# Products of q and the state in four quarters of the TensorE array, with the outputs of a chunk in two PSUM banks

## The chip, the cores and the metric

The kernel runs on one core of a Trainium2 chip. The metric is the device time of one execution in microseconds (us). In the rows below the engines are PE (TensorE matmuls), PEld (TensorE weight loads), DVE (VectorE), ACT (ScalarE), POOL (GpSimd) and SP (SyncE, which issues most DMAs). Each engine works through its own instructions in order; semaphores make one wait for another.

## The reference, cut to what matters

Three stages follow each other. Only the first is touched by the change.

```python
# 1. recurrent attention: B=4 batches, H=8 heads, S=768 steps, D=48
for t in range(S):
    state = alpha[t][:, None] * state + outer(k[t], v[t])   # D x D for each batch and head
    y[t] = q[t] @ state
x = y.transpose(0, 2, 1, 3).reshape(3072, 384)
# 2. x @ w_in (384 x 2048), a leaky rectifier, @ w_out
# 3. ((x @ w1) * (x @ w2)) @ w3 @ w_out2
```

## The kernel before

**Chunks.** The 768 steps of a batch are cut into 6 chunks of 128, so there are 24 chunks, numbered 0 to 23. Inside a chunk the recurrence becomes matrix products. With q and k scaled by the running products of alpha (`prep`), the kernel forms for each head the 128 x 128 scores (`scores`), masks them on DVE (`sc`), and then has y = v x scores + state x q (`yout`), and the update of the state, k transposed x v (`state`). The 8 heads lie as 4 pairs `p` of two heads `hh`: head 2p in partitions 0 to 63, head 2p + 1 in 64 to 127, 48 of each 64 in use. These products are plain float32, and each one shows in the trace as two MATMUL and two LDWEIGHTS instructions, so that a group of 8 products is a row with x16.

**The four groups of products of a chunk n**, in the order in which `chunk` writes them: `state` (tile `Up`, 8 products of 64 columns, contraction over 128 partitions, outputs of the two heads of a pair in the two halves of the partitions), `yout` (tile `yp`: 8 products of v and `sc`, 128 columns, same shape; then 8 products of the state `sst` and `qt`, contraction over the 64 partitions of a head, output in the same 64 partitions, which are a quarter of the array on its diagonal; these are left out in the first chunk of a batch, n = 0, 6, 12, 18), and `scores` of chunk n + 1 (tile `scp`, contraction over 48 partitions, 128 x 128 outputs, one PSUM bank for each `hh`). The last chunk of a batch (n = 5, 11, 17, 23) has no `state`. The transposes of k (`kT`, tile `kTp`) are a unit of their own.

**PSUM banks.** Of the 8 banks two hold `h` of stage 2, and two rings of three are for the rest. While stage 2 accumulates tile T (512 tokens, 4 chunks) in one ring, the attention of tile T + 1 uses the other, whose banks `bank` gives out in turn. Before, a chunk takes five: `Up` one, `yp` one, `scp` two, `kTp` one. A bank is free again when its reader is done: `Up` is read by DVE (`tmp`, or `sst` in the first chunk of a batch), `yp` by ACT (the copy to `yT`), `scp` by DVE (`sc`), `kTp` by ACT (the copy to `kT`). At the end of a tile ACT copies the three accumulators out (`x1e`).

**Order.** Stage 2 runs in steps of 9 matmuls of `G1` (tile `h`) and 9 of `G2` (tile `acc`). After each `G1`, ACT makes `u` from `h`, DVE makes `g`, ACT makes `gs` from `g`, DVE the second half of `gs`. `attend` spreads the units of attention between the steps. Among ACT's other work are `top` (the upper halves of the weights of a later stage, which waits for a DMA into `raw`), and `r` twice (logarithm and exponential of `prep`, of which the first waits for DVE's scan of `al`). A scheduler sets the order of PE, ACT and DVE; `tight` keeps the products of a chunk in the order written, except that the first after `untie` is free to move. Tile 0 (chunks 0 to 3) is done ahead of stage 2; chunks 4 to 7 run beside stage 2 of tile 0, up to about 98 us, and chunks 8 to 23 beside the tiles after it, up to about 432 us. Stage 3 fills the rest and has no attention in it.

**Output.** ACT copies `yp` into `yT`, DMAs place its rows in the layout of x (`place`), and the host orders the rows of w_in to fit.

Of the kernel before, what the change touches and what calls it, by code (L numbers as in the profile page):

```python
# [24 lines left out]
CH = 128  # L25
NC_B = S // CH
NSTEP = B * NC_B
NP = H // 2
# [35 lines left out]
def fused_kernel(ctx, tc, qk, al, vv, wf, ws, m_alpha, ident, maskn, out):  # L64
# [6 lines left out]
    def copy(out, in_):  # L71
        act.activation(out=out, in_=in_, func=AF.Copy)  # L72
# [172 lines left out]
    def ends(n):  # L245
        return n % NC_B == NC_B - 1
# [28 lines left out]
    pairs = [(p, hh, slice(64 * hh, 64 * hh + DP)) for p in range(NP) for hh in range(2)]  # L275

    def state(n, w):
        if ends(n):
            return
        t, v, end = st.pop(("kT", n)), st["v", n], st.pop(("pend", n))  # L280
        ps = bank([128, NP, DP], "Up", w)
        for p, hh, r in pairs:
            mm(ps[r, p], t[:, p, r], v[:, 2 * p + hh], start=True, stop=True)
        new = sst[(n + 1) % 2]
        pend = end.to_broadcast([128, NP, DP])
        if n % NC_B == 0:
            dve.scalar_tensor_tensor(out=new, in0=ps, scalar=-1.0, in1=pend, op0=ALU.mult, op1=ALU.mult)
        else:
            tmp = ap2.tile([128, NP, DP], F32, tag="tmp", name="tmp", bufs=1)
            dve.tensor_tensor(out=tmp, in0=sst[n % 2], in1=ps, op=ALU.subtract)  # L290
            dve.tensor_tensor(out=new, in0=tmp, in1=pend, op=ALU.mult)

    def yout(n, w):
        qt, v = st.pop(("qt", n)), st.pop(("v", n))
        sc = [st.pop(("sc", n, hh)) for hh in range(2)]
        alone = n % NC_B == 0
        ps = bank([128, NP, CH], "yp", w)
        for p, hh, r in pairs:
            mm(ps[r, p], v[:, 2 * p + hh], sc[hh][:, p], start=p == 0, stop=alone and p == NP - 1,
                      skip_group_check=True)  # L300
        if not alone:
            for p, hh, r in pairs:
                mm(ps[r, p], sst[n % 2][r, p], qt[r, p], start=False, stop=p == NP - 1, skip_group_check=True)
        T, c = divmod(n, SPT)
        if c % 2 == 0:
            st["yT"] = ap2.tile([128, NP, 2, CH], F32, tag="yT", name="yT", bufs=1)
        y = st["yT"]
        copy(y[:, :, c % 2], ps)
        if c == 0:
            new_x(T)  # L310
        if c % 2 == 0:
            return
        x = f32(xt[T][:, 1, :, (c - 1) * CH:(c + 1) * CH])
        y = y.rearrange("p a c t -> p a (c t)")

        def place():
            q = (sp, act) if n == SPT - 1 else (sp, sp)
            for hh in range(2):
                q[hh].dma_start(out=x[hh * D:(hh + 1) * D], in_=y[64 * hh:64 * hh + D, :KD])
            for i, (k, to, hh, e, n_) in enumerate(PIECES):  # L320
                q[i % 2].dma_start(out=x[to:to + n_, k], in_=y[64 * hh + e:64 * hh + e + n_, KD])

        later(1, place)
# [10 lines left out]

    def chunk(n, w, more=True):
        untie()
        state(n, w)
        yout(n, w)
        if more:
            scores(n + 1, w)  # L340
        load_v(n + 3)
# [282 lines left out]
    with tc.If(bad > 0):  # L624
        with tc.tile_pool(name="fa", bufs=1) as fa:
# [5 lines left out]
            with tc.For_i(0, B, 1) as b:  # L631
                dve.memset(S_, 0.0)
                with tc.For_i(0, NC_B, 1) as c:
# [7 lines left out]
                    for g in range(CH // TG):  # L641
# [21 lines left out]
                            pe.matmul(yp, blk, z.rearrange("p a e -> p (a e)"), start=True, stop=True)  # L663
                            copy(yt[:, i].rearrange("p a e -> p (a e)"), yp)
                        dst = y_d[one][:, :, g * TG:(g + 1) * TG]
                        whole = [(k, hh * D, hh, 0, D, k) for k in range(KD) for hh in range(2)]
                        for k, to, hh, e, n_, a in whole + [piece + (KD,) for piece in PIECES]:
                            sp.dma_start(out=dst[:, :, :, k, to:to + n_].rearrange("b c t e -> (b c) t e"),
                                         in_=yt[hh:hh + 1, :, a, e:e + n_])

        with tc.tile_pool(name="fb", bufs=1) as fb:
            wi = fb.tile([128, NF, KD, 128], F32, name="wi")
# [95 lines left out]
```

## Time and profile before

| | us |
|---|---|
| three runs | 861.25, 860.70, 860.72 |
| median | 860.72 |
| the profiled execution | 860.4 |
| its span (first to last instruction) | 858.5 |
| PE busy in the span | 832.5 |
| DVE busy | 459.3 |
| ACT busy | 352.6 |

The profiled execution lies 0.3 us under the median, and 1.9 us of it lie around the span. The page has the busy time of each engine and the chain of work that ended last. Timelines give the instructions in order of time, merged into rows where equal ones follow each other; the time in brackets is how long the engine stood idle ahead of a row, and what released it.

### The profile page before, as it was taken

The page shows a single profiled execution, that of the slowest core. Times are in us where ns is not written, and L with a number is a line of the kernel's source. Part 1 is how long each engine was busy: PE and PEld are TensorE (multiplying, and loading weights), DVE is VectorE, ACT ScalarE, POOL GpSimd, SP SyncE. Part 2 cuts the span into 40 slices and gives each one's busy share as a digit, 9 for nine tenths or more (in the row PEclk, how much of TensorE's full clock was granted, in tenths as well). Part 3 has the DMA queues.
Part 4 walks back from the last instruction along what each step waited for, and adds up shares of the span by engine and source line. Part 5 has one row for each costly group of instructions (what it writes and reads, how often), then busy time and mean ns, then how long its engine had stood idle before and what let it go on. Part 6 is the DMA issues. An engine that isn't in the chain of part 4 may idle for free.

```text
span 858.5 us, 11862 instructions
## 1 busy us (share of the span) xinstructions
PE 832.5 (97%) x4754; PEld 685.2 (80%) x4758; DVE 459.3 (53%) x643; ACT 352.6 (41%) x538; POOL 11.9 (1%) x53
## 2 busy tenths in 40 slices
PE   7698999999999999999999999999999999999996
PEld 4477788888888888888888889988888888888884
DVE  7889974675576577656434734551433435322221
ACT  4456765444454545454335634421313232222221
POOL 1100000000000000000000000000000000000000
PEclk9989999999999999999999999999999999999998
DMA  8665662421573476436002405430312104010101
GB/s 311 186 227 203 210 214 79 139 80 54 213 245 107 147 251 228 158 102 213 13 19 92 141 0 192 143 108 1 106 41 74 74 14 134 1 37 0 37 1 41
DMA packets 48623, 99.55 MB, mean 116 GB/s; under 512 B 4784, under 2 KB 25008, under 8 KB 48560
## 3 DMA queue, kind: packets, MB, share of 16 engines
q1 hardware_dynamic: 48320, 98.52, 34.1%
q8 instruction: 39, 0.64, 0.3%
q10 hardware_dynamic: 240, 0.20, 0.1%
q14 instruction: 24, 0.20, 0.1%
HBM read 75.63 MB, written 18.35 MB: 109 GB/s over the span
## 4 chain that ended last, share of the span: by engine, by line
PE 89%; DVE 5%; DMA 3%; ACT 1%; issue 1%; SPq 1%; DVEq 0%; ACTq 0%
PE ab L361 23%; PE h L361 21%; PE acc L361 11%; PE acc L386 8%; PE acc L387 7%; PE acc L389 7%; PE w L361 4%; PE yp L237 3%; PE scp L237 2%; PE Up L237 1%; DMA raw<-in_ws_dram 1%; DMA raw<-in_wf_dram 1%; PE kTp L256 1%; DVE y L146 1%; DVE al L214 1%
## 5 line engine op out<-in xcount | busy, mean ns | idle before, releaser
L361 PE MATMUL h<-x,w 128*128 128x512 f32 x864 | 215.3, 393 | 5.5 <-ACT x L72 5.5
L361 PE MATMUL ab<-x,w 128*128 128x512 f32 x864 | 203.7, 389 | 0.0
L361 PEld LDWEIGHTS h<-x,w 128*128 128x128 f32 x864 | 162.5, 189 | 39.9 <-ACT x L72 6.0
L361 PEld LDWEIGHTS ab<-x,w 128*128 128x128 f32 x864 | 162.1, 188 | 33.6
L386 PE MATMUL acc<-gs,w 128*128 128x512 f32 x288 | 114.6, 398 | 0.0
L564 DVE TENSOR_TENSOR c<-ab,a 128x512 f32<-128x512 f32 x48 | 33.1, 691 | 149.0 <-PE ab L361 149.0
L387 PE MATMUL acc<-gs,w 128*128 128x512 f32 x288 | 112.4, 390 | 0.0
L375 DVE SCALAR_TENSOR_TENSOR g<-h,salpha,u 128x512 f32<-128x512 f32 x96 | 71.8, 748 | 71.0 <-ACT u L373 70.5
L373 ACT ACTIVATE u<-h,sgn 128x512 f32<-128x512 f32 x96 | 65.5, 682 | 103.4 <-PE h L361 103.3
L361 PE MATMUL acc<-cs,w 128*128 128x512 f32 x432 | 105.8, 389 | 0.0
L378 DVE SCALAR_TENSOR_TENSOR gs<-g,sgn,gs 128x512 fp32r<-128x512 f32 x96 | 72.0, 750 | 50.3 <-ACT gs L377 49.5
L361 PEld LDWEIGHTS acc<-cs,w 128*128 128x128 f32 x432 | 81.0, 188 | 17.2 <-DVE cs L567 0.4
L377 ACT ACTIVATE gs<-g,sgn 128x512 fp32r<-128x512 f32 x96 | 69.0, 719 | 52.9 <-DVE g L375 52.9
L389 PE MATMUL acc<-gs,w 128*128 128x512 f32 x288 | 81.0, 389 | 0.0
L72 ACT ACTIVATE a<-ab 128x512 f32<-128x512 f32 x48 | 28.8, 599 | 113.7 <-PE ab L361 113.7
L72 ACT ACTIVATE cs<-c 128x512 fp32r<-128x512 f32 x48 | 30.2, 630 | 89.7 <-DVE c L564 89.7
L386 PEld LDWEIGHTS acc<-gs,w 128*128 128x128 f32 x288 | 54.0, 188 | 12.3 <-issue 0.2
L389 PEld LDWEIGHTS acc<-gs,w 128*128 128x128 f32 x288 | 54.1, 188 | 11.4
L387 PEld LDWEIGHTS acc<-gs,w 128*128 128x128 f32 x288 | 54.1, 188 | 10.6
L72 ACT ACTIVATE top<-raw 128x768 f16<-128x768 bf16 (+1 forms) x39 | 41.8, 1072 | 42.2 <-DMA raw<-in_ws_dram 25.6
L567 DVE TENSOR_TENSOR cs<-c,cs 128x512 fp32r<-128x512 f32 x48 | 33.2, 692 | 30.8 <-ACT cs L72 30.8
L146 DVE SCALAR_TENSOR_TENSOR y<-raw,top 128x768 int32<-128x768 int32 (+1 forms) x39 | 36.9, 947 | 8.9 <-ACT top L72 6.0
(64 smaller groups left out, 654.7 us busy)
## 6 DMA issues: line engine op xcount, KB each, us to landing
raw<-in_ws_dram SPq DMA_DIRECT2D x22, 767.8 KB, 5.7
qk<-in_qk_dram SPq DMA_DIRECT2D x24, 512.0 KB, 5.9
raw<-in_wf_dram SPq DMA_DIRECT2D x16, 767.8 KB, 5.8
ws_d<-y SPq DMA_DIRECT2D x22, 384.0 KB, 2.8
al<-in_al_dram SPq DMA_DIRECT2D x24, 256.0 KB, 5.0
v<-in_vv_dram SPq DMA_DIRECT2D x24, 256.0 KB, 3.0
alx<-in_al_dram SPq DMA_DIRECT2D x8, 768.0 KB, 4.6
x_d<-x1e SPq DMA_DIRECT2D x18, 256.0 KB, 5.0
```

The costliest lines, as they stand in the source:

```text
L72: act.activation(out=out, in_=in_, func=AF.Copy)
L146: return dve.scalar_tensor_tensor(out=y, in0=t[:, :, 0], scalar=13, in1=z[:, :n], op0=ALU.logical_shift_right, op1=ALU.bitwise_or)
L237: ins = pe.matmul(*a, **k)
L361: pe.matmul(ps, w, x, start=first and i == 0, stop=last and i == n - 1)
L373: act.activation(out=u, in_=ps, func=AF.Identity, scale=sg)
L375: dve.scalar_tensor_tensor(out=gt, in0=ps, scalar=sa, in1=u, op0=ALU.mult, op1=ALU.max)
L377: act.activation(out=s[:, 0], in_=gt, func=AF.Identity, scale=sg)
L378: dve.scalar_tensor_tensor(out=s[:, 1], in0=gt, scalar=sg, in1=f32(s[:, 0]), op0=ALU.mult, op1=ALU.subtract)
L386: pe.matmul(acc[T][m], r_out[f][:, 0, c], s[:, 0], start=f == 0, stop=False)
L387: pe.matmul(acc[T][m], r_out[f][:, 1, c], s[:, 0], start=False, stop=False)
L389: pe.matmul(acc[T][m], r_out[f][:, 0, c], s[:, 1], start=False, stop=f == NF - 1)
L567: dve.tensor_tensor(out=s[:, 1], in0=c, in1=f32(s[:, 0]), op=ALU.subtract)
```

## The change

`yout` now comes ahead of `state` in a chunk. Its outputs take two banks of the ring instead of one: bank `hh` holds the outputs of the heads `hh` of all four pairs, pairs 0 and 2 in the lower half of the partitions, 1 and 3 in the upper (`a` is the half). The products of the state and q come first; each contracts over the 64 partitions of its head and writes to the half `a`, and the four of two pairs are one in each quarter of the array. The products of v and the scores follow, first all of bank 0, then all of bank 1. ACT's one copy of `yp` (512 columns) becomes two of 256 columns. A chunk thus takes six banks of the ring of three instead of five: `yp` two, `Up` one, `scp` two, `kTp` one, so that within a chunk `scp` follows `yp` in the same two banks, and `kTp` follows `Up`. The DMAs of `place` are as many as before; which head stands in which row of x, and the host's order of w_in, change with it.

```diff
     def state(n, w):
+        v, end = st.pop(("v", n)), st.pop(("pend", n))
         if ends(n):
             return
-        t, v, end = st.pop(("kT", n)), st["v", n], st.pop(("pend", n))
+        t = st.pop(("kT", n))
...
     def yout(n, w):
-        qt, v = st.pop(("qt", n)), st.pop(("v", n))
+        qt, v = st.pop(("qt", n)), st["v", n]
...
-        ps = bank([128, NP, CH], "yp", w)
-        for p, hh, r in pairs:
-            mm(ps[r, p], v[:, 2 * p + hh], sc[hh][:, p], start=p == 0, stop=alone and p == NP - 1,
-                      skip_group_check=True)
+        ps = [bank([128, NP // 2, CH], "yp", w) for _ in range(2)]
+        half = [slice(64 * a, 64 * a + DP) for a in range(2)]
         if not alone:
-            for p, hh, r in pairs:
-                mm(ps[r, p], sst[n % 2][r, p], qt[r, p], start=False, stop=p == NP - 1, skip_group_check=True)
+            for i in range(NP // 2):
+                for hh, a in ((0, 0), (1, 1), (0, 1), (1, 0)):
+                    mm(ps[hh][half[a], i], sst[n % 2][half[hh], 2 * i + a], qt[half[hh], 2 * i + a], start=i == 0, stop=False,
+                       skip_group_check=True)
+        for hh in range(2):
+            for i in range(NP // 2):
+                for a in range(2):
+                    pr = 2 * i + a
+                    mm(ps[hh][half[a], i], v[:, 2 * pr + hh], sc[hh][:, pr], start=alone and i == 0, stop=i == NP // 2 - 1,
+                       skip_group_check=True)
...
-        copy(y[:, :, c % 2], ps)
+        for hh in range(2):
+            copy(y[:, 2 * hh:2 * hh + 2, c % 2], ps[hh])
...
     def chunk(n, w, more=True):
         untie()
+        yout(n, w)
         state(n, w)
-        yout(n, w)
         if more:
             scores(n + 1, w)
```

The order that the scheduler gives moves with it. On PE, chunk 13 (the second of tile 3), before:

```order
L361 MATMUL h<-x,w_84 128x512 x9
L237 MATMUL Up<-v,kT 64x64 [waits DVE_49,Activation_49]
L237 MATMUL Up<-v,kT 64x64 x7
L237 MATMUL yp<-sc,v 64x128 [waits DVE_49]
L237 MATMUL yp<-sc,v 64x128 x7
L237 MATMUL yp<-qt,sst_113 64x128 x8
L237 MATMUL scp<-qt,kn 128x128 [waits PE_49]
L237 MATMUL scp<-qt,kn 128x128 [waits DVE_49]
L237 MATMUL scp<-qt,kn 128x128 x6
L386 MATMUL acc_2193<-gs,w_82 128x512
```

and with the change, at the same place:

```order
L369 MATMUL h<-x,w_84 128x512 x9
L237 MATMUL yp<-qt,sst_113 64x128 [waits DVE_49] x2
L237 MATMUL yp<-qt,sst_113 64x128 x6
L237 MATMUL yp<-sc,v 64x128 x8
L237 MATMUL Up<-v,kT 64x64 [waits Activation_49]
L237 MATMUL Up<-v,kT 64x64 x7
L237 MATMUL scp<-qt,kn 128x128 [waits Activation_49]
L394 MATMUL acc_2219<-gs,w_82 128x512
L237 MATMUL scp<-qt,kn 128x128 [waits Activation_49]
L237 MATMUL scp<-qt,kn 128x128 x6
```

The products of q and the state moved to the front, the second product of `scp` waits for ACT and no longer for DVE, and one matmul of `acc` stands between the first and the second of `scp`. This form, one of `scp`, one of `acc`, seven of `scp`, stands in chunks 9, 10, 13, 15, 19, 21 and 22 of 8 to 23; in chunk 14 two, and in chunk 18 one, of `acc` stand ahead of all 8 of `scp`.

On ACT, in chunk 13, before and then with the change:

```order
L72 ACTIVATE top<-raw 128x768 [waits DMAHW1_49,DVE_49]
L373 ACTIVATE u<-h,sgn 128x512 [waits PE_49,Activation_49]
L377 ACTIVATE gs<-g,sgn 128x512 [waits DVE_49]
L72 ACTIVATE yT<-yp 128x4x128 [waits PE_49]
L72 ACTIVATE top<-raw 128x768 [waits DMAHW6_49,DVE_49,Activation_49]
```

```order
L72 ACTIVATE top<-raw 128x768 [waits DMAHW1_49,DVE_49]
L381 ACTIVATE u<-h,sgn 128x512 [waits PE_49,Activation_49]
L72 ACTIVATE yT<-yp 128x2x128 [waits PE_49]
L385 ACTIVATE gs<-g,sgn 128x512 [waits DVE_49]
L72 ACTIVATE yT<-yp 128x2x128 [waits PE_49]
L72 ACTIVATE top<-raw 128x768 [waits DMAHW6_49,DVE_49,Activation_49]
```

The one copy became two, with `gs` between them; `top` and `u` stand ahead of both as they stood ahead of the one. In chunks 15, 19 and 22 it is `u`, copy, `gs`, copy, without a `top` right ahead; in 9 and 10 `r` twice stands ahead of `u`; in 14 it is `top`, `u`, `r`, `r`, `gs` and then both copies; in 21 `gs`, `top`, `u`, copy, `gs`, copy.

On PE, chunk 16 (the first of tile 4), before and then with the change:

```order
L361 MATMUL h<-x,w_83 128x512 x3
L237 MATMUL Up<-v,kT 64x64 [waits Activation_49]
L237 MATMUL Up<-v,kT 64x64 x7
L237 MATMUL yp<-sc,v 64x128 [waits Activation_49]
L237 MATMUL yp<-sc,v 64x128 x7
L237 MATMUL yp<-qt,sst_112 64x128 x8
```

```order
L369 MATMUL h<-x,w_83 128x512 x3
L237 MATMUL yp<-qt,sst_112 64x128 [waits Activation_49]
L369 MATMUL h<-x,w_83 128x512
L237 MATMUL yp<-qt,sst_112 64x128 [waits Activation_49]
L237 MATMUL yp<-qt,sst_112 64x128 x6
L237 MATMUL yp<-sc,v 64x128 x8
```

One matmul of `h` moved in between the first and the second product of q and the state. Chunks 8 and 20, the first of tiles 2 and 5, have the same; in all of these the two copies of `yp` follow right behind the three of `x1e` on ACT.

## Rows read from the trace of the kernel before

**Rows 1.** The page: busy time of PE and DVE, and the chain that ended last, by engine.

```profile
PE 832.5 (97%) x4754; PEld 685.2 (80%) x4758; DVE 459.3 (53%) x643; ACT 352.6 (41%) x538; POOL 11.9 (1%) x53
...
PE 89%; DVE 5%; DMA 3%; ACT 1%; issue 1%; SPq 1%; DVEq 0%; ACTq 0%
```

**Rows 2.** Busy time of each engine by stretch: the attention of tile 1 (56 to 98 us), and of tiles 4 and 5.

```profile
56.00:98.00 42.00, 37.82 (x283) 30.28 (x283) 39.66 (x57) 26.03 (x37) 2.54 (x7) 1.00 0.68 236
...
270.00:432.00 162.00, 161.77 (x1052) 132.83 (x1051) 97.51 (x139) 76.50 (x112) 2.08 (x10) 1.00 0.47 157
```

The columns are the stretch, its length, busy us and instructions of PE, PEld, DVE, ACT and POOL, the granted clock, the DMA share and GB/s.

**Rows 3.** Timeline of PE over chunk 13: start, length until the last end, what.

```profile
227.30 1.07 PE L361 MATMUL h<-x,w 128*128 128x512 f32 x4
228.30 0.69 PE L237 MATMUL Up<-v,kT 128*64 128x64 f32 x16
228.82 1.05 PE L237 MATMUL yp<-sc,v 128*64 128x128 f32 x16
229.79 1.09 PE L237 MATMUL yp<-qt,sst 64*64 64x128 f32 x16
230.81 1.16 PE L237 MATMUL scp<-qt,kn 48*128 48x128 f32 x16
231.91 0.50 PE L386 MATMUL acc<-gs,w 128*128 128x512 f32 x1
232.24 0.40 PE L387 MATMUL acc<-gs,w 128*128 128x512 f32 x1
232.48 0.39 PE L386 MATMUL acc<-gs,w 128*128 128x512 f32 x1
```

**Rows 4.** Timeline of PE in chunk 6, where the group of `scp` is cut after its first product (x2) by matmuls of `acc`.

```profile
76.31 0.49 PE L237 MATMUL scp<-qt,kn 48*128 48x128 f32 x2
76.73 0.50 PE L386 MATMUL acc<-gs,w 128*128 128x512 f32 x1
...
79.42 1.16 PE L237 MATMUL scp<-qt,kn 48*128 48x128 f32 x14 [1.96 <-DVE sst L287]
80.50 0.50 PE L386 MATMUL acc<-gs,w 128*128 128x512 f32 x1
```

**Rows 5.** Waits of PE from 45 to 440 us: who waited for whom, us in total, times, the longest.

```profile
PE scp L237 <- DVE sst L287: 2.0, 1, 2.0
...
PE scp L237 <- DVE tmp L290: 0.9, 2, 0.7
```

**Rows 6.** Groups of ACT instructions by line and shape: busy us, mean ns of one, idle time ahead.

```profile
L72 ACT ACTIVATE yT<-yp 128x512 f32<-128x512 f32 x24 | 14.0, 585 | 14.3 <-PE yp L237 9.1 <-DMA x<-yT 5.1
...
L72 ACT ACTIVATE x<-x 128x768 fp32r<-128x768 f32 x12 | 10.1, 840 | 2.2 <-DMA x<-yT 1.7 <-issue 0.4
```

**Rows 7.** Chunk 19: the first row of its PE group, and ACT's timeline beside it.

```profile
345.98 0.69 PE L237 MATMUL Up<-v,kT 128*64 128x64 f32 x16
...
346.14 0.69 ACT L373 ACTIVATE u<-h,sgn 128x512 f32<-128x512 f32 x1 [0.85 <-PE h L361]
347.83 0.72 ACT L377 ACTIVATE gs<-g,sgn 128x512 fp32r<-128x512 f32 x1 [1.00 <-DVE g L375]
```

**Rows 8.** ACT's timeline in chunk 13.

```profile
230.05 1.07 ACT L72 ACTIVATE top<-raw 128x768 f16<-128x768 bf16 x1 [3.42 <-DMA raw<-in_ws_dram]
230.98 0.66 ACT L373 ACTIVATE u<-h,sgn 128x512 f32<-128x512 f32 x1
232.46 0.72 ACT L377 ACTIVATE gs<-g,sgn 128x512 fp32r<-128x512 f32 x1 [0.82 <-DVE g L375]
233.09 0.58 ACT L72 ACTIVATE yT<-yp 128x512 f32<-128x512 f32 x1
```

**Rows 9.** Chunk 10: PE's first and last group of it, and ACT's timeline.

```profile
172.25 0.69 PE L237 MATMUL Up<-v,kT 128*64 128x64 f32 x16
...
174.76 1.45 PE L237 MATMUL scp<-qt,kn 48*128 48x128 f32 x16
...
174.39 0.67 ACT L373 ACTIVATE u<-h,sgn 128x512 f32<-128x512 f32 x1
175.88 0.72 ACT L377 ACTIVATE gs<-g,sgn 128x512 fp32r<-128x512 f32 x1 [0.82 <-DVE g L375]
```

**Rows 10.** Chunk 9: PE's first group, and ACT's timeline.

```profile
159.80 0.69 PE L237 MATMUL Up<-v,kT 128*64 128x64 f32 x16
...
162.31 0.72 ACT L377 ACTIVATE gs<-g,sgn 128x512 fp32r<-128x512 f32 x1 [0.82 <-DVE g L375]
```

**Rows 11.** Chunk 14: PE's first group, and ACT's timeline.

```profile
244.84 0.69 PE L237 MATMUL Up<-v,kT 128*64 128x64 f32 x16
...
245.61 0.66 ACT L373 ACTIVATE u<-h,sgn 128x512 f32<-128x512 f32 x1
...
247.66 0.71 ACT L377 ACTIVATE gs<-g,sgn 128x512 fp32r<-128x512 f32 x1
```

**Rows 12.** Chunk 21: PE's first group and the two parts of `scp`, and ACT's timeline.

```profile
391.20 0.69 PE L237 MATMUL Up<-v,kT 128*64 128x64 f32 x16
...
393.71 0.48 PE L237 MATMUL scp<-qt,kn 48*128 48x128 f32 x2
394.43 1.16 PE L237 MATMUL scp<-qt,kn 48*128 48x128 f32 x14 [0.23 <-DVE tmp L290]
...
391.61 1.08 ACT L72 ACTIVATE top<-raw 128x768 f16<-128x768 bf16 x1 [3.63 <-DMA raw<-in_ws_dram]
```

More of the change, by code (lines that the diff above doesn't have):

```diff
@@ L665, in fused_kernel @@
                         dst = y_d[one][:, :, g * TG:(g + 1) * TG]
-                        whole = [(k, hh * D, hh, 0, D, k) for k in range(KD) for hh in range(2)]
-                        for k, to, hh, e, n_, a in whole + [piece + (KD,) for piece in PIECES]:
+                        whole = [(k, a * D, a, 0, D, k) for k in range(KD) for a in range(2)]
+                        for k, to, a, e, n_, g_ in whole + [piece + (KD,) for piece in PIECES]:
+                            hh, pr = g_ // 2, 2 * (g_ % 2) + a
                             sp.dma_start(out=dst[:, :, :, k, to:to + n_].rearrange("b c t e -> (b c) t e"),
-                                         in_=yt[hh:hh + 1, :, a, e:e + n_])
+                                         in_=yt[hh:hh + 1, :, pr, e:e + n_])
         with tc.tile_pool(name="fb", bufs=1) as fb:
@@ L736 @@
     order = np.empty((KD, 128), dtype=np.int64)
-    order[:, :2 * D] = np.arange(KD * 2 * D).reshape(KD, 2 * D)
-    for k_, to, hh, e, n in PIECES:
-        order[k_, to:to + n] = KD * 2 * D + hh * D + e + np.arange(n)
+    head = [[4 * (g % 2) + 2 * a + g // 2 for a in range(2)] for g in range(NP)]
+    for k_ in range(KD):
+        for a in range(2):
+            order[k_, a * D:(a + 1) * D] = head[k_][a] * D + np.arange(D)
+    for k_, to, a, e, n in PIECES:
+        order[k_, to:to + n] = head[KD][a] * D + e + np.arange(n)
     w_in = np.asarray(inputs["moe_w_in"])[order.reshape(-1)].reshape(KD, 128, NF, 128).transpose(2, 1, 0, 3).reshape(NF, 128, DM)
```

## The prediction

> **What bounds the kernel now.** I read the page first. PE is busy for 97% of the span, and 89% of the chain that ended last is PE [rows 1], so time on PE is time of the kernel, unless a stretch has another limit. The busy times by stretch show one that has: from 56 to 98 us DVE is busy for 39.7 of 42 us and PE idles, while from 270 to 432 us PE works 161.8 of 162 us [rows 2]. So I count what the change does in chunks 8 to 23, which lie behind 98 us, in full, and treat chunks 0 to 7 apart. Next come PE's timelines. Chunk 13 is the plain case: four groups of products, `Up` 0.52 us, v and scores 0.97, state and q 1.02, `scp` 1.10, each from its start to that of the next, with no idle time [rows 3]. PE waited for `scp` in few places, always for DVE to read the bank of `Up` [rows 5]. Last, ACT's timelines, because with the change it is ACT that sets the banks of `scp` free.
>
> **How long a group takes.** `scp` with one product (x2) takes 0.42 us, with seven (x14) 1.08 [rows 4], with eight 1.10 [rows 3]. One product can't overlap with itself; its two instructions are two rounds. Eight products on two parts of the array are eight rounds. So a round is (1.10 - 0.42) / 6 = 0.11 us, and 0.19 goes into starting and ending a group of that shape. That x14 takes as long as x16 fits: seven products are four on one part and three on the other.
>
> **State and q in four quarters.** Eight rounds become four if the four parts work at once: 1.02 - 4 x 0.11 = 0.58 us, 0.44 less. The trace has no four at once. The bounds are 1.02 (the two banks or the shared partitions make it no faster) and 0.58. I take 0.58, for the rows show two outputs in halves of one bank at full rate (`yp`) and two contractions over half the rows into two banks at full rate (`scp`) [rows 3], and a quarter is the two together. 14 of the chunks 8 to 23 have these products (not 12 and 18): -14 x 0.44 = -6.2 us.
>
> **Cut groups.** Where one `acc` stands behind the first of `scp`, the one product costs 0.42 us by itself, the group left over is shorter by only 0.02 [rows 3, 4], and PE changes its shape twice more. A change costs 0.09 us behind (the first `acc` takes 0.33 to the next, the second 0.24) and 0.08 ahead (`h` x4 from 227.30 at some 0.23 each has its last start at 227.99; `Up` follows 0.31 later) [rows 3]. Together 0.42 - 0.02 + 0.17 = 0.57 us, in seven chunks: +4.0. The state products cut by one `h` in 8, 16 and 20: one product is two rounds, 1.02 - 6 x 0.11 = 0.36, and 0.17 for the changes: 3 x 0.53 = +1.6. In 14 and 18 only the changes: +0.3. The four groups otherwise follow each other in as many changes of shape as before, at no cost.
>
> **The new wait.** `scp` now needs the two banks of `yp` in the same chunk, so its first product waits for ACT's first copy and its second for the second. Queued behind on PE is everything: six more of `scp`, then stage 2. Counted from a chunk's start t, PE would be ready for the seven products of `scp` at t + 0.58 + 1.49 (`yp` and `Up`) + 0.42 + 0.33 + 0.08 = t + 2.90. The second copy stands behind `gs` on ACT, which needs `g` from DVE, which needs `u`; `gs` starts 1.48 us behind `u` [rows 8]. A copy of 512 columns takes 0.585, one of 768 another 0.84 [rows 6], so some 1.0 ns a column, and one of 256 is estimated at 0.35 (bounds 0.29, half of the 0.585, and 0.585). I take ACT's times from the trace of before, since what stands ahead is the same.
>
> - Chunk 13: ACT sat until 230.05 for `top`'s DMA, so `gs` ends at 232.46 + 0.72 = 233.18 [rows 8] and the second copy at 233.55; PE is ready at 228.30 + 2.90 = 231.20: 2.35 us of wait.
> - Chunk 10: `r` twice delays `u`; `gs` ends at 176.60, copy 177.0, PE 172.25 + 2.90 = 175.15 [rows 9]: 1.85.
> - Chunk 9: `gs` ends at 163.03, copy 163.4, PE 162.70 [rows 10]: 0.7.
> - Chunk 14: both copies behind `gs`, which ends at 248.37, so 249.1; PE ready after two `acc` at t + 2.07 + 0.65 = 247.56 [rows 11]: 1.5.
> - Chunk 21: `top` from 391.61, `u` some 392.6, `gs` 394.1 to 394.8, copy 395.2; PE 394.1 [rows 12]: 1.1.
> - Chunks 15, 19, 22: nothing ahead of `u`; in 19 the copy ends at 348.95, PE is ready at 348.88 [rows 7]: 0.1 each.
> - Chunks 8, 12, 16, 20 have no `gs` between the copies; the second ends about when `Up` does: 0.15 each. 11 and 17 have no `Up`, and only the second product waits, for the first copy: 0.15 each.
>
> Sum of waits: 2.35 + 1.85 + 0.7 + 1.5 + 1.1 + 0.3 + 0.6 + 0.3 = 8.7 us. From this goes what `scp` waited there before for `Up`'s bank: 0.28 in chunk 10 (1.45 against 1.16 in length [rows 3, 9]) and 0.70 in 21 (its x14 ends its 1.08 at 395.51 instead of 394.81 [rows 4, 12]): -1.0. ACT's additional 24 x 0.12 us lie in its idle time (41% busy [rows 1]), apart from those counted.
>
> [...] The rows show that copying is not what PE waits for now [rows 5]. [...]
>
> **Chunks 0 to 7.** DVE's work is the same, and it sets the pace [rows 2]. In the opening `sst` and the weights behind it on DVE come later, as `Up` goes last; in tile 1 `scp` no longer waits for `sst`. I take 0, bounds -2.7 (the waits of 2.0 and the longest of 0.7 for `sst` and `tmp` gone, both in tile 1 [rows 4, 5]) and +1.5: `Up` starts later in a chunk by the length of `yp`, 0.97 + 0.58 = 1.55 us, and the `sst` that DVE makes of it may come as much later once, where DVE has nothing else to do; afterwards DVE is the engine that is full and doesn't pass it on [rows 2].
>
> **The sum.** -6.2 + 4.0 + 1.6 + 0.3 + 8.7 - 1.0 = +7.4 us. On the profiled 860.4 that is 867.8, and with the 0.3 by which the median of the runs lies above it, 868.1.
>
> **Rivals.** *The copies come in time.* If DMAs, scan and `u` shift so that ACT reaches the second copy by t + 2.90, the 8.7 are gone, and so are the 2.7 in tile 1: 860.7 + 7.4 - 8.7 - 2.7 = 856.7. It decides from waits under some 0.3 us in each of 9, 10, 13, 14 and 21. For it: the scheduler put an `acc` there to fill the gap, and a later PE lets DMAs catch up. Against it: `top` and `r` stand ahead by order, and their DMAs are issued at a pace that follows the chunks. Half of it, with 4.4 us of waits left and the 2.7 gained, gives 861.1, no change that can be told.
>
> *The quarters don't overlap.* Then the change doesn't do what it says: each group keeps 1.02. In the five chunks with long waits the 0.44 would hide, in nine not: +4.0, 872.1. For it: no row has four at once. Against it: the halves do overlap in both directions.
>
> *Slower copies.* At 0.585 each the second copy is 0.24 later in some ten chunks: +2.4, 870.5. It belongs to the forecast's range.
>
> **How the numbers follow.** A measurement of this kernel tells about 0.2% (1.7 us) from no change. The forecast, ACT's copies late, has 0.63 (863 to 871); the copies in time 0.18; the half-way case 0.13; no overlap 0.06. So faster 0.18, same 0.13, slower 0.69. The range leaves out the copies in time, and reaches from a little under the half-way case to no overlap: 860 to 872. The predicted time is 868.1.
>
> **What would show it.** State and q take about 0.58 us in 14 places; `scp` waits for ACT `yT`, some 8 to 9 us in all behind 98 us, longest in chunk 13; the waits of `scp` for `sst` and `tmp` are gone. A group of 1.0 us for state and q would make the second rival right, waits for `yT` under 2 us the first. The prediction fails in size if `top` or `r` come at other times than in the trace of before.

## The result and the profile after

| | median, us | runs | range, us |
|---|---|---|---|
| before | 860.71 | 4 | 859.96 to 861.25 |
| with the change | 875.22 | 4 | 869.38 to 877.99 |

The change makes the kernel slower: the ratio of the times is 1.0145, with a 95% interval of 1.0119 to 1.0172. The forecast of slower was right and its size was not: 868.1 us was forecast, and 875.2 lies outside the range of 860 to 872. The four executions also spread over 8.6 us, where the four of before agreed within 1.3; on the chips of the later experiments the kernel before spreads over 3.4 to 5.2 us as well.

The profiled execution took 876.1 us, with a span of 874.3. The page shows the chain that ended last [rows 1] with less PE, and with more of DMA and ACT on it:

```profile
PE 841.5 (96%) x4754; PEld 688.3 (79%) x4758; DVE 460.9 (53%) x643; ACT 355.1 (41%) x562; POOL 11.6 (1%) x53
...
PE 84%; DMA 5%; DVE 4%; ACT 3%; issue 2%; SPq 1%; ACTq 0%; DVEq 0%
```

The waits of PE from 45 to 440 us, the same view as [rows 5] (who waited for whom, us in total, times, longest): the waits for `sst` and `tmp` are gone, and eleven waits for ACT's copies stand in their place, 11.2 us of them. A third wait of before, for DVE's `kn`, is not among the lines of [rows 5]; it went from 1.9 us (the first line here) to 0.3.

```profile
PE scp L237 <- DVE kn L232: 1.9, 2, 1.6
```

```profile
PE scp L237 <- ACT yT L72: 11.2, 11, 2.5
PE scp L237 <- DVE kn L232: 0.3, 1, 0.3
```

Chunk 13 on PE, the place of [rows 3]. State and q (`yp<-qt,sst`) take 0.60 us to the start of the next group, where they took 1.02. `scp` then waits 1.40 us for the first copy and 0.63 for the second, and what follows it runs at half speed: x14 takes 1.60 us to the next start instead of 1.08, and the `acc` behind it 0.59 instead of 0.33.

```profile
236.44 0.67 PE L237 MATMUL yp<-qt,sst 64*64 64x128 f32 x16
237.04 1.09 PE L237 MATMUL yp<-sc,v 128*64 128x128 f32 x16
237.97 0.63 PE L237 MATMUL Up<-v,kT 128*64 128x64 f32 x16
240.00 0.49 PE L237 MATMUL scp<-qt,kn 48*128 48x128 f32 x2 [1.40 <-ACT yT L72]
240.41 0.49 PE L394 MATMUL acc<-gs,w 128*128 128x512 f32 x1
241.54 1.67 PE L237 MATMUL scp<-qt,kn 48*128 48x128 f32 x14 [0.63 <-ACT yT L72]
243.14 0.79 PE L395 MATMUL acc<-gs,w 128*128 128x512 f32 x1
```

ACT beside it, as in [rows 8]: it sits 3.33 us in front of `top` until a DMA has landed, and `u`, the first copy, `gs` and the second copy follow in that order. A copy of 256 columns takes 0.37 us.

```profile
238.08 1.07 ACT L72 ACTIVATE top<-raw 128x768 f16<-128x768 bf16 x1 [3.33 <-DMA raw<-in_ws_dram]
239.02 0.65 ACT L381 ACTIVATE u<-h,sgn 128x512 f32<-128x512 f32 x1
239.57 0.37 ACT L72 ACTIVATE yT<-yp 128x256 f32<-128x256 f32 x1
240.49 0.72 ACT L385 ACTIVATE gs<-g,sgn 128x512 fp32r<-128x512 f32 x1 [0.55 <-DVE g L383]
241.12 0.36 ACT L72 ACTIVATE yT<-yp 128x256 f32<-128x256 f32 x1
```

The busy times by stretch, with the columns of [rows 2], show what the forecast had no term for. The granted clock (the third number from the end) is 1.00 in most of the attention and lower, 0.53 to 0.66 in the mean, in four stretches, each of which begins in or just behind a place where PE stood idle for `scp` (chunks 4, 7, 9 and 13):

```profile
58.00:65.00 7.00, 6.81 (x28) 5.63 (x29) 5.97 (x10) 3.64 (x6) 0.00 (x0) 0.53 0.56 204
...
98.00:103.00 5.00, 5.00 (x28) 4.00 (x26) 4.16 (x8) 1.06 (x2) 0.19 (x1) 0.66 0.69 228
...
170.00:174.00 4.00, 4.00 (x18) 3.08 (x15) 1.87 (x4) 0.00 (x0) 0.38 (x2) 0.57 0.36 94
...
242.00:246.00 4.00, 4.00 (x20) 3.21 (x17) 3.68 (x6) 1.33 (x2) 0.29 (x2) 0.57 0.62 198
246.00:440.00 194.00, 191.01 (x1250) 155.29 (x1249) 119.33 (x169) 92.61 (x144) 2.24 (x15) 1.00 0.47 161
```

What a stretch loses is its length times what is missing to 1.00: 7 x 0.47 = 3.3, 5 x 0.34 = 1.7, 4 x 0.43 = 1.7 and 1.7, 8.4 us in all. Before, the clock was 1.00 from 56 to 98 and from 270 to 432 us [rows 2], and in the two stretches between:

```profile
98.00:150.00 52.00, 52.00 (x233) 43.10 (x232) 34.41 (x46) 33.65 (x47) 0.11 (x1) 1.00 0.46 154
150.00:270.00 120.00, 120.00 (x893) 98.62 (x893) 79.71 (x118) 55.77 (x86) 2.44 (x16) 1.00 0.42 137
```

Where the 15.8 us between the spans arose, from the start of the first product of chunks 8, 12, 16 and 20 in the two timelines, and the end:

| | before | changed | later by |
|---|---|---|---|
| chunk 8 | 150.37 | 155.07 | 4.7 |
| chunk 12 | 219.90 | 227.92 | 8.0 |
| chunk 16 | 301.25 | 313.82 | 12.6 |
| chunk 20 | 381.78 | 395.79 | 14.0 |
| end | 858.5 | 874.3 | 15.8 |

Up to chunk 8 it is 4.7 us, and the two falls of the clock there lose 5.0, while PE's waits in chunks 4 to 7 add up to much the same in both (4.6 and 5.0 us). Behind it it is 11.1, and the two falls lose 3.4; the other 7.7 compare with the +7.4 of the sum.

### The profile page after: what moved, and what is told of

Read it like the earlier page. It is cut to its first block, busy times and chain, and to the rows that moved or that the text cites. A ratio compares the mean times of both kernels' runs of the same rounds, so it can differ in the third digit from the quotient of the medians.

```text
span 874.3 us, 11859 instructions
## 1 busy us (share of the span) xinstructions
PE 841.5 (96%) x4754; PEld 688.3 (79%) x4758; DVE 460.9 (53%) x643; ACT 355.1 (41%) x562; POOL 11.6 (1%) x53
## 4 chain that ended last, share of the span: by engine, by line
PE 84%; DMA 5%; DVE 4%; ACT 3%; issue 2%; SPq 1%; ACTq 0%; DVEq 0%
PE ab L369 22%; PE h L369 20%; PE acc L369 11%; PE acc L395 7%; PE acc L394 7%; PE acc L397 7%; PE w L369 4%; DMA raw<-in_ws_dram 2%; PE scp L237 2%; PE yp L237 2%; DMA raw<-in_wf_dram 2%; DMA al<-in_al_dram 1%; DVE al L214 1%; PE kTp L256 1%; SPq L329 1%
## 5 line engine op out<-in xcount | busy, mean ns | idle before, releaser
L369 PE MATMUL h<-x,w 128*128 128x512 f32 x864 | 219.0, 397 | 4.5 <-ACT x L72 4.5
L394 PE MATMUL acc<-gs,w 128*128 128x512 f32 x288 | 116.3, 404 | 0.0
L395 PE MATMUL acc<-gs,w 128*128 128x512 f32 x288 | 115.5, 401 | 0.0
L397 PE MATMUL acc<-gs,w 128*128 128x512 f32 x288 | 81.6, 392 | 0.0
L395 PEld LDWEIGHTS acc<-gs,w 128*128 128x128 f32 x288 | 55.3, 192 | 12.2 <-issue 0.4
L394 PEld LDWEIGHTS acc<-gs,w 128*128 128x128 f32 x288 | 55.1, 191 | 12.2 <-issue 0.3
L397 PEld LDWEIGHTS acc<-gs,w 128*128 128x128 f32 x288 | 55.0, 191 | 12.0
L237 PE MATMUL scp<-qt,kn 48*128 48x128 f32 x384 | 35.7, 298 | 14.8 <-ACT yT L72 12.2
```

The source lines that it names most:

```text
L237: ins = pe.matmul(*a, **k)
L369: pe.matmul(ps, w, x, start=first and i == 0, stop=last and i == n - 1)
L394: pe.matmul(acc[T][m], r_out[f][:, 0, c], s[:, 0], start=f == 0, stop=False)
L395: pe.matmul(acc[T][m], r_out[f][:, 1, c], s[:, 0], start=False, stop=False)
L397: pe.matmul(acc[T][m], r_out[f][:, 0, c], s[:, 1], start=False, stop=f == NF - 1)
```

## The experiments

Theory A: `scp` waits for ACT's copies, which stand behind work that waits itself, and behind waits that are long enough the granted clock falls; waits, cuts and clock are the whole loss, and the four quarters by themselves gain. Theory B, the rival: the products in quarters, or the new order with its changes of shape, cost the clock or the time themselves.

**again.** The changed kernel as it is, on the chip of the next three.

> The changed kernel as it is, as a yardstick for the others on this chip. Theory A (the waits of scp for the copies to yT are long enough that the granted clock falls to 0.5 behind some of them, and this is what the forecast of 868 lacked): 869 to 878 us, with stretches of some 3.4 us at 0.5 behind chunks 7, 9 and 13, each costing 1.7 us, and one of some 7 us behind chunk 5; executions differ by how many falls they have. Theory B (the clock falls because of the products in four quarters themselves, whatever waits): the same time, but falls also behind chunks that have these products and no wait, such as 10, 15 and 22.

Measured: 871.7 us (868.3 to 873.0), 1.0108 times before (1.0069 to 1.0147). The profiled execution (span 869.2) has its waits of `scp` for `yT` (7.8 us, nine of them) at other places, and the falls with them: none behind 4, 7 and 13, one behind 9, and one of some 7 us behind chunk 17, where `top` was late this time.

```profile
166.00:170.00 4.00, 4.00 (x17) 3.00 (x15) 1.71 (x4) 0.00 (x0) 0.37 (x2) 0.57 0.39 100
170.00:319.00 149.00, 147.24 (x988) 119.54 (x986) 93.06 (x132) 69.68 (x110) 2.05 (x14) 1.00 0.42 141
319.00:327.00 8.00, 7.21 (x27) 5.88 (x28) 6.09 (x8) 4.06 (x7) 0.10 (x1) 0.57 0.99 345
```

(The expectation books the first wait of tile 1 under chunk 5; the timeline has it in chunk 4.) No fall stands behind a chunk without a wait, as A says. The falls moved, though the program is the same, so they differ from one execution to the next. They are not the whole of the spread: the four executions of the result, at 876.1, 874.3, 878.0 and 869.4 us, have mean granted clocks of 0.984, 0.980, 0.987 and 0.988, so the slowest lost less to the clock than the profiled one. On this chip the kernel before spread over 5.2 us and the changed one over 4.8.

**fill.** PE gets useless work where it would wait.

```diff
+FILL = (7, 9, 13)
...
-        for p, hh, r in pairs:
-            mm(ps[r, p], t[:, p, r], v[:, 2 * p + hh], start=True, stop=True)
+        for _ in range(6 if n in FILL else 1):
+            for p, hh, r in pairs:
+                mm(ps[r, p], t[:, p, r], v[:, 2 * p + hh], start=True, stop=True)
```

> The products of state in chunks 7, 9 and 13 are issued six times over (48 instead of 8, the same results), so that PE has work while scp waits there for ACT. Useless work of 3 x 5 x 0.42 = 6.3 us, most of it inside waits of 2.0, 2.4 and 2.8 us. Theory A (idle PE loses the clock): the falls to 0.5 behind 7, 9 and 13 are gone, 3 x 1.7 = 5.1 us less, and the cut of scp in 9 and 13 is gone as well (2 x 0.57): some 869 us where the unchanged kernel takes 875. Theory B (the products in quarters lose the clock): the falls stay, and the time is that of the unchanged kernel or up to 1 us above it.

Measured: 874.9 us (874.2 to 879.5), 3 us above `again`, so the saving of some 6 us was missed. The clock did what A says: it is 1.00 behind chunks 7, 9 and 13.

```profile
90.00:160.00 70.00, 70.00 (x480) 58.00 (x478) 50.47 (x69) 42.88 (x63) 0.59 (x4) 1.00 0.51 173
160.00:230.00 70.00, 69.84 (x549) 57.54 (x548) 42.67 (x62) 29.74 (x50) 1.18 (x8) 1.00 0.25 78
230.00:400.00 170.00, 167.86 (x1171) 136.93 (x1169) 110.11 (x155) 83.44 (x129) 2.36 (x16) 1.00 0.55 183
404.00:411.00 7.00, 6.54 (x26) 4.95 (x26) 4.36 (x8) 2.06 (x3) 0.19 (x1) 0.53 0.32 99
```

But the fillers took 2.34 us each (`Up` takes 2.90 to the start of `scp` instead of 0.56), 7.0 and not 6.3, and where `top` comes early they cover little: in `again` chunk 13 waited only 0.6 us. Chunk 21, not filled, lost 3.3 us of clock (404 to 411). As a way to save time it is refuted; on the clock it speaks for A, though `again` had no fall behind 7 and 13 either, so that only chunk 9 tells.

**order_only.** The order of the change without its quarters and banks.

```diff
+        yout(n, w)
         state(n, w)
-        yout(n, w)
```

with the products of `sst` first in `yout`, into the one bank and the quarters of before.

> The kernel before with only the order of the change: yout ahead of state, state and q ahead of v and scores, but the old diagonal quarters, one bank and one copy of 512 columns. State and q take 1.02 us again in 14 chunks (+6.2 against the change); scp still waits for the one copy to yT behind gs, the copy ends 0.24 later and PE comes 0.44 later. Theory A: waits of scp for yT of 6 to 10 us behind 98 us, falls of the clock behind the longest, 870 to 878 us. Theory B (quarters take the clock): no fall behind 56 us, 860.4 + 4.0 of cuts + some 7 of waits = 869 to 872 us.

Measured: 872.2 us (867.9 to 876.9), ratio 1.0103 (1.0057 to 1.0148). There are no new quarters here, and waits and falls are there all the same:

```profile
PE scp L237 <- ACT yT L72: 7.3, 5, 2.1
```

```profile
236.00:240.00 4.00, 4.00 (x21) 3.25 (x20) 3.87 (x7) 1.14 (x2) 0.22 (x2) 0.57 0.91 281
...
338.00:342.00 4.00, 4.00 (x22) 3.20 (x19) 3.36 (x6) 1.48 (x3) 0.19 (x1) 0.59 0.75 308
...
410.00:414.00 4.00, 4.00 (x12) 3.08 (x11) 1.81 (x4) 0.88 (x1) 0.19 (x1) 0.57 0.37 94
```

They follow chunks 13, 18 and 21, each with a wait of `scp` for `yT`. So the new quarters are not needed for the falls; the new order, the other half of B, is still in this run. The order alone, which puts `scp` behind a copy on ACT, costs about as much as the whole change.

**copy_dve.** The second copy on DVE.

```diff
-        for hh in range(2):
-            copy(y[:, 2 * hh:2 * hh + 2, c % 2], ps[hh])
+        copy(y[:, :2, c % 2], ps[0])
+        dve.tensor_copy(out=y[:, 2:, c % 2], in_=ps[1])
```

> The changed kernel with the second copy of yp on DVE instead of ACT, so that the second product of scp waits no longer for a copy behind gs. Theory A (the copies behind gs are the loss): waits for yT behind 98 us fall to about 3 us (14: 1.4, 13: 0.8, 10: 0.3), cuts of scp behind 98 us to one chunk, no falls of the clock behind 98 us: 860.4 - 6.2 + 1.6 + 0.3 + 0.6 + 3 = 859.7, and with 4 copies of 0.4 on the full DVE in tile 1 some 861 us (858 to 866). Theory B (quarters take the clock): the falls behind 98 us stay and the time is 865 to 870.

Measured: 874.7 us (872.4 to 879.6); the expected 861 was far off. The second copy was not the main cause: the first one is late too, because `top` and `r` stand ahead of both, and DVE's copy brings waits of its own. The clock still falls behind 98 us: it is 0.50 from 324 to 327 us, behind a wait of some 2.5 us in chunk 17, and 0.986 in the mean of the profiled execution.

```profile
PE scp L237 <- ACT yT L72: 5.9, 6, 2.5
...
PE scp L237 <- DVE yT L316: 1.7, 3, 0.8
```

**top_pool.** `top` of the later blocks is copied by POOL, where the new argument of `upper` is true.

```diff
-            upper(top, raw[i + 1])
+            upper(top, raw[i + 1], i + 1 >= NF)
```

> The changed kernel with the copies `top` of the later blocks (those that ACT makes beside the attention of tiles 2 to 5) on POOL, which is nearly idle. Theory A (scp waits for the copies to yT because ACT sits in front of `top` until its DMA has landed, with u and both copies queued behind): the waits in 13, 17 and 21 are gone, some 4 to 5 us, and the falls of the clock behind them; 9 and 10, where r stands ahead, stay. Against the 872 to 875 us of the unchanged change: 866 to 869 us. Theory B (the engine order itself, second copy behind gs, is enough to make scp late): each of these chunks still waits 0.6 us or more, in sum under 2 us gained, 871 to 874 us.

Measured: 868.5 us (868.1 to 868.8), ratio 1.0075 (1.0056 to 1.0095). Chunk 13 has no wait left, only its cut:

```profile
233.67 0.64 PE L241 MATMUL Up<-v,kT 128*64 128x64 f32 x16
234.23 0.49 PE L241 MATMUL scp<-qt,kn 48*128 48x128 f32 x2
...
235.08 1.16 PE L241 MATMUL scp<-qt,kn 48*128 48x128 f32 x14
```

17 and 21 lost theirs as well, and from chunk 16 on this kernel loses nothing more on the one before (8.4 us behind it at the start of chunk 16, 7.9 at the end of the span). What remains is in 9 and 14, where `r` stands ahead of the copies and waits for DVE's scan of `al`. In chunk 14 of this run:

```profile
251.96 0.63 ACT L232 ACTIVATE r<-al 128x512 f32<-128x512 f32 x1 [2.20 <-DVE al L218]
...
253.16 0.70 ACT L389 ACTIVATE gs<-g,sgn 128x512 fp32r<-128x512 f32 x1
253.77 0.64 ACT L72 ACTIVATE yT<-yp 128x256 f32<-128x256 f32 x2
```

Theory A forecast 866 to 869, theory B 871 to 874, so A holds, with `top` as a part of the cause. The ratio's interval overlaps that of `again`; what shows it is the trace.

**before_top_pool.** The same in the kernel before.

> The same move of `top` to POOL in the kernel before, as a control. There PE never waits for ACT's copies behind 98 us, so both theories expect 860 to 861.5 us, within 0.2% of the kernel before; if it gains 3 us or more, `top` on ACT costs time by another way than the new wait.

Measured: 859.7 us (858.7 to 860.6), ratio 0.9972 (0.9958 to 0.9986). `top` on ACT cost the kernel before some 2 us, a little more than was expected and less than the 3 that would have spoken for another way. In its profiled execution `scp` waits for `sst` in chunk 6 as in [rows 4], 2.0 us, and here the clock does fall, to 0.51 from 78.5 to 85.5 us; its mean over the execution is 0.990, where the kernel before has 0.993. This kernel has neither the order nor the quarters of the change, so a fall needs neither.

**state_between** and **between_top_pool.** The first copy gets a start over `scp`: Q, half of V, `Up`, the other half of V, with the banks in that order; then also `top` on POOL.

```diff
+        up = None if ends(n) else bank([128, NP, DP], "Up", w)
...
         for hh in range(2):
+            if hh:
+                state(n, up)
             for i in range(NP // 2):
```

> The changed kernel with the products of state between the products of v and scores of bank 0 and those of bank 1, and the banks given out in that order: scp then needs the bank of the first copy and that of Up, kTp that of the second copy. The first copy may start 1.0 us before scp is ready, and stands ahead of gs on ACT in most chunks; the scheduler cuts scp in one chunk instead of seven. Theory A (the second copy behind gs, and `top` ahead of u, are the loss): cuts -6 x 0.57, waits for yT behind 98 us some 4 us (13, 17, 21 and where r stands ahead), state and q at 0.6: 860.4 - 6.2 + 0.6 + 1.9 + 4 = 860.7 with no fall of the clock, 861 to 866 with one to three. Theory B (what costs is the change of shape and the quarters): no better than 870.

> Both: state between, and `top` on POOL. Theory A: hardly a wait for yT behind 98 us is left (1 to 2 us), no fall of the clock behind 98 us: 860.4 - 6.2 + 0.6 + 1.9 + 1.5 = 858.2 us, with tile 1 uncertain by 2: 856 to 861, faster than the kernel before or equal to it. Theory B: 866 or more.

Measured: 870.2 us (868.9 to 874.1) and 866.3 (863.0 to 870.1), ratios 1.0103 (1.0069 to 1.0137) and 1.0051 (1.0029 to 1.0073). Neither came down to its forecast by A; both lie where B put them. `scp` is cut less often, but now it needs the bank of `Up` soon after `Up`, and waits for `tmp` on DVE; the first of the two in these waits from 98 to 440 us:

```profile
PE scp L237 <- ACT yT L72: 3.8, 4, 2.8
PE scp L237 <- DVE tmp L290: 3.0, 4, 1.0
```

In both orders tried, a ring of three banks that gives out six in a chunk makes `scp` wait for somebody. In between_top_pool the clock stays at 1.00 behind 98 us, and without its waits the way from chunk 8 to chunk 23 takes 278.3 us, as before (278.0): this order, with v and scores in two parts, takes back what the quarters give. To that extent B is right.

**share** and **share_top_pool.** So five banks again: `Up` goes into the unused half of the second bank of `yp`. `scp` then takes the free bank and that of the first copy.

```diff
-        ps = [bank([128, NP // 2, CH], "yp", w) for _ in range(2)]
+        ps = [bank([128, NP // 2, CH], "yp", w)]
+        both = bank([128, 2, NP // 2, CH], "ypU", w)
+        ps.append(both[:, 0])
...
             copy(y[:, 2 * hh:2 * hh + 2, c % 2], ps[hh])
+            if not hh:
+                state(n, up)
```

> The changed kernel with Up in the unused half of the second bank of yp, so that a chunk takes five banks again: scp takes the bank that is free and that of the first copy, whose products are done 1.0 us (v and scores of the second bank, Up) before scp is ready; no product waits for the second copy but kTp. Theory A (the loss is scp's wait for the second copy, the cuts that come with it and the clock lost behind the waits): scp is cut only in chunk 14; waits for yT stay where `top` holds the first copy up (13, 17, 21: 2 to 3 us): 860.4 - 6.2 + 1.6 + 0.6 + 2.5 = 858.9 us, with at most one fall of the clock 860.6. Theory B (four quarters, more changes of shape or the order Q V U S cost the time): 866 or more.

> The same with `top` of the later blocks on POOL. Theory A: the first copy is in time in 13, 17 and 21 too: 860.4 - 6.2 + 1.6 + 0.6 + 0.5 = 856.9 us (855 to 859), below the kernel before and below the kernel before with `top` on POOL (859.7). Theory B: 865 or more.

Measured: 869.4 us (866.0 to 873.7) and 868.1 (866.3 to 870.7), ratios 1.0076 (1.0052 to 1.0101) and 1.0069 (1.0049 to 1.0088). Both missed A's forecast and lie where B put them. In the second, `scp` waits three times from 98 to 440 us, all for a copy behind `r` (chunks 9, 10 and 14), with a fall of the clock of some 7 us in and behind the last (0.983 in the mean of the profiled execution). Where there is neither wait nor cut, the chunks are as short as hoped: in chunk 13 the four groups take 3.18 us (232.26 to 235.44) instead of the 3.61 of before [rows 3].

```profile
PE scp L241 <- ACT yT L72: 6.6, 3, 3.8
```

**tied** and **tied4.** Order the copies ahead of `r`, and `tmp` ahead of the scan.

```diff
+    def tie(n, ins):
+        if n >= 2 * SPT:
+            tc.keep_in_program_order(ins)
...
-            copy(y[:, 2 * hh:2 * hh + 2, c % 2], ps[hh])
+            tie(n, copy(y[:, 2 * hh:2 * hh + 2, c % 2], ps[hh]))
...
-        act.activation(out=r, in_=Pv, func=AF.Ln)
+        tie(n - 2, act.activation(out=r, in_=Pv, func=AF.Ln))
```

and the same for `tmp` and the scan; in tied4 from `n >= SPT` on.

> Up shares the second bank of yp, `top` of the later blocks on POOL, and from chunk 8 on the copies of yp stand on ACT ahead of the first r of prep of a later chunk, and tmp ahead of its scan on DVE, so that neither r nor a late DMA of al can stand ahead of a copy that scp waits for. scp is then whole in all chunks but 11, in most of them behind nine acc, which fill the time until the copy. Theory A: no wait of scp for yT behind 98 us, no fall of the clock there; state and q at 0.60 save 14 x 0.42 = 5.9, three cuts of them cost 1.6, the changes of shape around the nine acc 8 x 0.17 = 1.4: behind 98 us some 3 us less than the kernel before; in front of it 1.5 us more, as with the shared bank alone: 859 us (857 to 861). Theory B (quarters or a longer chain of changes cost the time by themselves): 866 or more.

> The same from chunk 4 on, where DVE sets the pace. Theory A: the wait of scp in chunk 7 (1.2 us) goes too, or comes back as a wait of sc for DVE; within 1.5 us of the run tied, 857 to 861 us. Theory B: 866 or more.

Measured: 881.9 us (879.5 to 886.6) and 885.2 (882.3 to 890.2), the slowest of all, and far above A's 857 to 861. With `r` late, `kn` is late, and `scp` needs `kn`: from 98 to 450 us the wait has only moved.

```profile
PE scp L246 <- DVE kn L241: 12.7, 9, 3.5
PE scp L246 <- ACT yT L72: 1.7, 2, 1.1
```

Here too the clock falls behind the long waits (0.57 from 240 to 248 us, in and behind a wait of 2.89 us in chunk 13), and these are for DVE, so the falls are not tied to waits for ACT.

**early_al** and **before_early_al.** What `r` waits for in the end is a DMA (in share_top_pool DVE sits 1.90 us ahead of the scan in chunk 14 until the DMA of `al` has landed), so that DMA goes a chunk earlier: three buffers of `al` instead of two, on top of share_top_pool; and the control, the kernel before with the same and `top` on POOL.

```diff
-    albuf = [ap1.tile([128, NP, CH + 1], F32, name=f"al{i}") for i in range(2)]
+    albuf = [ap1.tile([128, NP, CH + 1], F32, name=f"al{i}") for i in range(3)]
...
+            sp.dma_start(out=albuf[n % 3][:, :, 1:], in_=al[b, c])
...
+        load_al(n + 1 if n >= 2 else NSTEP)
...
-        sp.dma_start(out=albuf[n % 2][:, :, 1:], in_=al[b, c])
...
-            dve.tensor_tensor(out=tmp, in0=sst[n % 2], in1=ps, op=ALU.subtract)
+            dve.tensor_tensor(out=new, in0=sst[n % 2], in1=ps, op=ALU.subtract)
```

> Up shares the second bank of yp, `top` of the later blocks on POOL, and the DMA of al runs a chunk earlier, with three buffers instead of two (tmp is written in place into the new state to make room); kn stays as early as before. Theory A (what is left of the loss in share_top_pool, 4 us in chunks 9, 10 and 14 and the clock behind 14, is ACT's r behind a scan that waits for al): these waits shrink under 1 us each, no fall of the clock behind 98 us, and 14 x 0.42 of state and q come through, less 1.6 for three cut groups: 856 to 861 us. Theory B (r stands ahead of the copies whatever al does, or the quarters cost the time by themselves): 865 or more.

> The control: the kernel before with `top` on POOL, al a chunk earlier and the state in place. Both theories: 858 to 861 us, as with `top` on POOL alone (859.7); early_al against this one gives what four quarters are worth by themselves, -4 us by theory A.

Measured: early_al takes 856.1 us (855.8 to 857.5), 0.9929 times the kernel before (0.9909 to 0.9949); the control takes 864.4 (860.7 to 866.4), ratio 1.0020 (1.0004 to 1.0036), more than the 858 to 861 expected of it. The control's trace has a wait of 1.31 us for `sst` in chunk 18 that early_al doesn't have, so the 8.2 us between the two are not all due to the quarters. The waits of PE in early_al from 45 to 440 us and the busy times show a kernel that hardly waits in its attention, at full clock (the wait for `x` is the start of stage 2):

```profile
PE h L382 <- ACT x L72: 5.5, 1, 5.5
PE yp L248 <- DVE sc L283: 1.2, 1, 1.2
PE scp L248 <- ACT yT L72: 0.8, 1, 0.8
```

```profile
49.00:440.00 391.00, 388.91 (x2607) 316.21 (x2607) 269.13 (x379) 186.48 (x298) 31.03 (x57) 1.00 0.47 159
```

Chunk 13 of it on PE. The first four products start within 0.02 us of each other, the next four 0.16 later: the four quarters do work at once. From 226.64 to the `acc` at 229.82 the groups take 3.18 us, against the 3.61 of before (228.30 to 231.91 [rows 3]).

```profile
226.64 0.32 PE L248 MATMUL yp<-qt,sst 64*64 64x128 f32 x1
226.65 0.32 PE L248 MATMUL ypU<-qt,sst 64*64 64x128 f32 x1
226.66 0.32 PE L248 MATMUL yp<-qt,sst 64*64 64x128 f32 x1
226.66 0.32 PE L248 MATMUL ypU<-qt,sst 64*64 64x128 f32 x1
226.80 0.27 PE L248 MATMUL yp<-qt,sst 64*64 64x128 f32 x1
...
228.73 1.16 PE L248 MATMUL scp<-qt,kn 48*128 48x128 f32 x16
229.82 0.50 PE L407 MATMUL acc<-gs,w 128*128 128x512 f32 x1
```

From the start of chunk 8 (149.95 us) to the end of the span (854.2) it is 704.2 us, where the kernel before takes 708.1 (858.5 - 150.37): 3.9 less. The terms: -14 x 0.42 = -5.9, and three groups of state and q that are still cut (+1.6) and one of `scp` (+0.6, chunk 17) give -3.7. The same stretch takes 706.2 us in before_top_pool and 710.2 in the control, so that by the kernel compared with it is 2.0 to 6.0 us less; -3.7 lies between. With this one run B falls for the time too, and for the clock, since order and quarters are both in it: without the waits, the quarters are worth about what the rounds say.

## Why the prediction was right in its direction and wrong in its size

- **Four quarters.** Right: 0.60 us instead of the forecast 0.58 in the 11 chunks behind 98 us where the group is whole, and the three cut ones came as booked under the next point; the rival in which the quarters don't overlap is refuted.
- **Cuts and changes of shape.** Right. Chunk 15, with the cut of `scp` and without a wait, takes 4.02 us (277.83 to 281.85), 0.24 of it for the `acc` inside; the 3.78 left are 0.60 above the 3.18 of uncut groups, forecast 0.57. Chunk 16, with state and q cut, takes 4.04 us, 0.23 of it for the `h` inside and 0.08 for a longer `scp`: 0.55 above, forecast 0.53.
- **The waits.** Right in kind and roughly in sum, not in place. Behind 98 us `scp` waited for `yT` 6.7 us in eight places, forecast 8.7. Chunk 13 waited 2.0 (forecast 2.35), 9 waited 1.7 (0.7), 21 waited 2.4 (1.1), 17 some 0.45 (0.15), and 10 and 14 hardly at all (1.85 and 1.5). The times of ACT were taken from the trace of before; `top` and `r` came at other times after, as the prediction warned, and do so again in every execution. Chunk 17 was booked as a wait for the first copy alone, but `top` stands ahead of that one too. One reading of the rows was wrong as well: before, `scp` waited not always for the bank of `Up`, but 1.9 us of its 4.8 for `kn`.
- **Missing: the clock.** This is the step that failed. The prediction let a wait cost its own length ("Sum of waits ... 8.7 us") and had no term for the clock. In the trace after, four waits are followed by stretches near 0.5, 8.4 us in all; 868.1 + 8.4 = 876.5 against the 876.1 of the profiled execution. Behind chunk 8 the sum without the clock held: 7.7 against 7.4. That it meets so closely is in part luck. From the start of chunk 8 to that of chunk 23, where both kernels have the same 1903 matmuls, the change adds 11.7 us: 6.4 of waits (6.7 less the 0.2 of before), 3.4 of clock, and 1.9 for quarters and cuts together, which the sum had at -6.2 + 5.9. The waits were 2.0 under their forecast, and the rest some 2 over it. The trace after has the falls at four waits (1.00 ahead of them, 0.53 to 0.66 in the stretches in and behind them), which took 2.5 us at most and 1.6 in chunk 7. The rows of before show none: the clock is 1.00 from 56 to 98 us [rows 2], which takes in the wait of 1.96 us of [rows 4].
- **Chunks 0 to 7.** "I take 0, bounds -2.7 and +1.5" was wrong for the same reason: 4.7 us, with 5.0 of clock. New waits of `scp` in chunks 4 and 7 were not forecast, since DVE was taken to set the pace there. In length they only took the place of the old ones; what was new is the clock behind them.
- **The range.** It took in neither the clock nor the spread of the executions. Only the fastest one (869.4) lay within it.
- **The copies.** The waits for `yT` stand where `scp` needs the banks that the copies free, but their cause is the queue ahead of the copies: a copy takes 0.37 us, and in early_al, with an earlier DMA and `top` elsewhere, 0.8 us of waits are left from 45 to 440 us, where the changed kernel had 11.2. In order_only they are there without the new quarters (7.3 us, five of them).

Shown: the waits behind `top` (top_pool), behind `r` and `al` (early_al), the gain of the quarters alone (early_al), falls without the new quarters (order_only) and without the new order (before_top_pool). Not separated: early_al shares a bank, moves `top` and brings `al` earlier all at once. Open: why some waits have a fall behind them and others none. In the changed kernel chunk 21 waited 2.4 us with none, as did `scp` for 1.96 before [rows 4], where before_top_pool has a fall behind the same wait; in another execution the falls of chunks 4, 7 and 13 were absent. No run here tells it.

## What to carry to other kernels

A faster group on the bound engine is worth its saving only if its new buffers come free in time; ask not how long the copy that frees them takes, but what stands ahead of it in its engine's queue, and which DMA that waits for. Count a new wait of PE as its length plus a possible loss of clock: here waits of 1.14 us (tied, chunk 7) to 2.89 us (tied, chunk 13) had stretches at a granted clock of 0.50 behind them that lost another 1.7 or 3.4 us, others of such a length had none, and one execution differed from the next. Look for room in the banks before reordering: two halves that share a bank kept the ring as it was, and then it was the inputs that had to come earlier.

## What was not expected of the hardware

- The granted clock fell from 1.00 to 0.50 behind idle stretches of PE as short as 1.6 us (the changed kernel, chunk 7; in tied 1.14 us, also chunk 7), stayed there for some 3.4 or 6.8 us, and lost 1.7 or 3.4 us each time. It fell behind waits for ACT (2.50 us, chunk 4 of the changed kernel) and for DVE (2.89, chunk 13 of tied) alike, and not behind all waits of the same length (none behind the 2.4 of chunk 21).
- ACT's two copies of 256 columns took 0.37 us each, 0.75 in all, against 0.585 for the one of 512 [rows 6].
- In chunk 13 of early_al four products with outputs in two banks started within 0.02 us; each part of the array started its next instruction 0.16 us later and those behind it 0.11, the length of a round.
